# An adaLN block on one core: a new instruction order from planned times, the first x loads on SyncE, a shorter warm-up, and the GpSimd normalisation as product and sum

## The chip, the cores and the metric

The kernel runs on one core of a Trainium2 chip. The metric is device time in microseconds, from the chip's own measurement, as a median over repeated runs. The profile records one execution: instructions by engine (PE is TensorE's matmuls, PEld its weight loads, DVE VectorE, ACT ScalarE, POOL GpSimd, SP SyncE), DMA activity, and the TensorE clock that was granted.

## The reference, cut to what matters

x has 2048 rows of D = 640 bf16 values; c is one row of 640 that conditions the whole block.

```python
mod = (silu(c) @ w_mod).reshape(1, 6, 1, 640)        # w_mod: 640 x 3840
sa, ca, ga, sb, cb, gb = (mod[:, i] for i in range(6))
h = layernorm(x) * (1 + ca) + sa
q, k, v = split_heads(h @ wqkv)                      # 32 heads of 20
p = softmax(where(0 <= i - j < 256, q @ k.T / sqrt(20), -1e9))
x = x + ga * ((p @ v) @ wo)
h = layernorm(x) * (1 + cb) + sb
out = x + gb * ((sigmoid(h @ w_gate) * (h @ w_up)) @ w_down)   # F = 1536
```

The attention is a sliding window: each row sees itself and the 255 rows before it.

## The kernel before, in words

The 2048 rows are worked in 8 chunks of 256 (CH), each of two blocks of 128 rows. The kernel doesn't write its instructions directly. Each piece of work is recorded as an operation with possible engines, an assumed duration and latency, what it reads and writes, a priority and a tag. `Prog.schedule` then places all operations: at each step it takes, for every engine, the earliest possible start, and among those that could start within a small margin of it (PE_EPS on TensorE) the one with the lowest priority number. The table PRI adds a correction by tag. `emit` writes the result: one fixed order per engine, with semaphore waits. On the chip every engine works strictly in that order, SyncE's DMA issues too.

**Conditioning.** c is loaded on ACT's queue, transposed by a small matmul (L624), and turned into silu(c) (L626 to L628). L630 copies it 128 columns wide into silubc. The slices of w_mod go through TensorE with silubc as operand: the first pair (shift and scale of the first layer norm) into tile S at the start (tag modA), the others later (modb, modc). They borrow the space of wd, wu and hh, so those weights can only be loaded afterwards.

**Warm-up.** Until the first modulation weights are there, TensorE runs matmuls on a zeroed buffer (L639, 9 groups of two), and single ones between the modA steps (`fill`, L650).

**First layer norm and projections.** x blocks 0 and 1 are loaded on ACT's queue behind c, all others on SyncE's. `ln_stats` computes mean and variance on VectorE (L741, L743), variance to the power -1/2 on GpSimd (L746, L748), and the normalised x on VectorE or GpSimd (L751). The result is transposed, for chunks 0 and 1 by TensorE (evicted with scale and shift, L786, L787) and afterwards by DMA transposes on SyncE (L757), then scaled and shifted in place (`modulate`, L765, L766, any of three engines). q, k and v come from 320-column matmuls (helper L658); q and k are evicted into stg (L812, L813) and transposed to QT and KT.

**Attention.** There are 90 score sets. A set (`score_set`) is 2048 score columns in the one tile S, four PSUM banks, computed in four strips of TensorE at once (L659), followed by one exponential of 2048 columns on ACT (L924) into one of eight E buffers and by masks on GpSimd (L932, L934). After the sets of half the heads of a chunk, `burst` does P·V into two of the four M banks; `norm` divides on VectorE (transposes L975, reciprocal L980, product L982, transpose L984). The result goes to DRAM (doc<-On) and back in another layout (oT<-doc), both on SyncE.

**Output projection and MLP.** `outproj` multiplies oT by wo, which was scaled by ga, adds x (L1038), and does the second layer norm, with DMA transposes into h2T. `mlp` does gate and up (L658), tanh on ACT (L1078), the product on VectorE (L1080), the down projection with wd scaled by gb, the residual add (L1099) and the store. All projections, P·V groups and MLP tiles share the four M banks.

The priorities let the order mix chunks: while chunk a's score sets run, TensorE's other work is projections of later chunks and output projection and MLP of earlier ones.

Of the kernel before, what the change touches and what calls it, by code (L numbers as in the profile page):

```python
# [8 lines left out]
ALU = mybir.AluOpType  # L9
# [71 lines left out]
class Prog:  # L81
# [3 lines left out]
    def __init__(self, nc):  # L85
        self.nc = nc
        self.ops = []
        self.seq = 0

    def op(self, eng, fn, dur, reads=(), writes=(), prio=50.0, lat=0.05, work=None, tmin=0.0, extra=(), tag="", hold=(),  # L90
# [10 lines left out]
        o.lat = lat  # L101
        o.prio = prio + PRI.get(tag, 0.0)
# [292 lines left out]
def c_pe(n):  # L395
# [3 lines left out]
PE_EPS = 0.117  # L399
PRI = {  # L400
    "amodu2": 349.1, "amodu3": 69.8, "amodu4": -2, "amodu5": 20.4, "amodu6": 21.9, "amodu7": 33.4, "apow0": -17.1,
    "apow1": -0.2, "apow2": -233.1, "apow3": -9.4, "apow4": -4.7, "apow5": -39.6, "apow6": -201.2, "apow7": 26.9,
    "astats1": 2, "astats2": -137.3, "astats3": 147.7, "astats4": 52, "astats5": 202.7, "astats6": 112.2,
    "astats7": -8.8, "atr3": -6.2, "atr4": -3.2, "atr5": -194.6, "atr6": 10.3, "atr7": -24.5, "axh0": -203,
    "axh2": -66.7, "axh3": 71.6, "axh4": -24.4, "axh5": 33.9, "axh6": -20.5, "axh7": 9.8, "bmodu0": -166.8,
    "bmodu1": 13.9, "bmodu2": 1.5, "bmodu3": 15.4, "bmodu4": -1.8, "bmodu5": 93.1, "bmodu6": 3.4, "bmodu7": -1.2,
    "bpow0": 4.3, "bpow1": 150.8, "bpow2": -11.8, "bpow3": -188.6, "bpow4": -35, "bpow5": 41.6, "bpow6": -22.5,
    "bpow7": -15.1, "bstats0": 20.1, "bstats1": 21.9, "bstats2": 16.8, "bstats3": 14.9, "bstats4": 25.8,
    "bstats5": -84.4, "bstats6": 22.4, "bstats7": -22.6, "btr0": -39.2, "btr1": -39.3, "btr2": -8.5, "btr3": 35,
    "btr5": -82, "btr6": 4.1, "btr7": -2.4, "bxh0": 24.8, "bxh1": -260.1, "bxh2": -55.1, "bxh3": 34, "bxh4": 72.4,  # L410
    "bxh5": 103.8, "bxh6": 81, "bxh7": 17.1, "divide_0": -16.1, "divide_1": 34.3, "divide_2": -154.9,
    "divide_3": 6.6, "divide_4": 14.8, "divide_5": -19.9, "divide_6": -11.9, "divide_7": 6.6, "down0": -15.1,
    "down1": -21.3, "down2": -20, "down4": 0.4, "down5": 1.9, "down7": 60.2, "evqk0": 16.1, "evqk1": 334.5,
    "evqk2": 27.2, "evqk3": 339.9, "evqk4": -0.3, "evqk5": 4.1, "evqk6": -33, "evqk7": -0.3, "evqt0": -11.6,
    "evqt1": -8.4, "evv0": 41.8, "evv1": 235.3, "evv2": 2.5, "evv3": -5.5, "evv4": -16.9, "evv5": -108.2,
    "evv6": -60.1, "evv7": -59.5, "exp0": -116.1, "exp1": -16.2, "exp2": -46.3, "exp3": 5.9, "exp4": -147.4,
    "exp5": -3.4, "exp6": 1.1, "exp7": -126.7, "glu_0": -1.3, "glu_1": 0.5, "glu_2": 26.7, "glu_3": -19.5,
    "glu_4": -37, "glu_5": -3.6, "glu_6": 8.5, "glu_7": 4.2, "hTe0": -31.6, "hTe1": 34.3, "mask0": 136.2,
    "mask2": -61.4, "mask3": 78.7, "mask4": -36.4, "mask5": -30.5, "mask6": 3.2, "mask7": 94.8, "mlpg0": -25,
    "mlpg1": -24.5, "mlpg2": -24, "mlpu0": -25, "mlpu1": -24.5, "mlpu2": -24, "modb": -25.7, "modc": -22.2,  # L420
    "n_ow_0": -20.3, "n_ow_1": -41.5, "n_ow_2": 44.8, "n_ow_3": 103.9, "n_ow_4": -5.8, "n_ow_5": -19.8,
    "n_ow_6": -1.4, "n_ow_7": 33.8, "oT_0": 17.5, "oT_1": 32.5, "oT_2": 12.6, "oT_3": 76.6, "oT_4": -64.2,
    "oT_5": 13.2, "oT_6": 2.6, "oT_7": 49.3, "out": 7.2, "projk0": -33.4, "projk2": 26.4, "projk3": -3.9,
    "projk4": 15.6, "projk5": 1.5, "projk6": 7.4, "projk7": 4, "projq0": -114.6, "projq2": 45.3, "projq3": -8.2,
    "projq4": 6.1, "projq5": -4, "projq6": 8.5, "projq7": -7.9, "projv0": -43.1, "projv1": 8.7, "projv2": 224.6,
    "projv4": -6, "projv5": 2.7, "projv6": 16.2, "projv7": 10.7, "ptr0": -337.9, "ptr1": -256.9, "pv0": -37.3,
    "pv1": -290.4, "pv2": -37.9, "pv3": -37.1, "pv4": -28.1, "pv5": -70.8, "pv6": -10.1, "pv7": -9.1, "qkt2": 7.9,
    "qkt3": 6.7, "qkt4": 64.8, "qkt5": -12.3, "qkt6": -3.6, "qkt7": -4.9, "qtr0": -154.4, "qtr1": -20.9,
    "recip_1": -1.9, "recip_2": 23.6, "recip_3": -2.4, "recip_4": 28.1, "recip_5": -22.7, "recip_6": 2.1,
    "recip_7": -9.2, "res1_0": -0.2, "res1_1": 5, "res1_2": 55.2, "res1_3": 7.6, "res1_4": 13.1, "res1_5": -5.3,  # L430
    "res1_6": -6.4, "res1_7": 11.2, "res2_0": 6.2, "res2_1": -29.9, "res2_2": -5.9, "res2_3": 1.7, "res2_4": -3.1,
    "res2_5": 40.9, "res2_6": -17.8, "res2_7": 2.6, "score0": -287.1, "score1": -347.7, "score2": -20.2,
    "score3": 1.8, "score4": -13.1, "score5": -50.5, "score6": -2.7, "score7": 11.5, "tanh_0": 29, "tanh_1": 20.7,
    "tanh_2": 23.5, "tanh_3": 22.7, "tanh_4": 26.2, "tanh_6": -2.3, "tanh_7": -20.3, "tr1_0": 19.8, "tr1_1": 6.2,
    "tr1_2": -28.1, "tr1_3": 15.6, "tr1_4": 45.4, "tr1_5": -90.8, "tr1_6": -19.7, "tr1_7": 5.2, "tr2_0": 204.6,
    "tr2_1": 224.6, "tr2_2": -128.4, "tr2_3": 42, "tr2_4": 64.5, "tr2_5": 40.4, "tr2_6": 0.1, "tr2_7": 27.5,
    "wd": -19.6, "wds": -7.7, "wg": 2.8, "wm2": -13.2, "wo": -20, "wo0": -2.2, "wo1": -12.2, "wo2": 9.1, "wo4": 10.8,
    "wo5": 28.7, "wo6": 6.6, "wo7": 30, "wos": -29.2, "x10": 529.8, "x11": 584.9, "x12": 476, "x13": 633,
    "x14": 745.4, "x15": 731.1, "x4": 394.6, "x5": 337, "x6": 375.5, "x7": 0.5, "x8": 473.6, "x9": 471.4, "y0": 10.9,
    "y1": 23.7, "y10": 8.6, "y11": 0.3, "y12": 0.2, "y13": 31.2, "y14": 1, "y15": 2.7, "y2": -0.2, "y3": 0.4,  # L440
    "y4": 24.5, "y5": 24.4, "y6": 15.9, "y7": -3, "y8": 23.9, "y9": 2,
}
TR1 = 2
# [4 lines left out]
PACE0 = -95.83  # L448
PACE = 0.103
AFTER = 0  # L450
LEAD = 2
FILL = 1
# [8 lines left out]
MOE = ('dve', 'act', 'pool')  # L461


def build(nc, A_x, A_wqkv, A_wo, B_x, B_w_gate, B_w_up, B_w_down, c, w_mod, out, S=2048):
# [50 lines left out]
    p_st = sbpool("st", 3, [128, 32], F32)  # L515
# [51 lines left out]
    def load_x(pool, b, prio, tmin=0.0, eng="sp"):  # L567
        t = Tile(pool, f"{pool.name}_{b}")
        dma(lambda: t.ap[:], lambda: x_flat[b * 128:(b + 1) * 128, :], 0.47 if b > 1 else 0.9, writes=[t.r()], prio=prio, tmin=tmin, tag=f"x{b}" if pool is p_x0 else f"y{b}",
            eng=eng, lat=0.05 if b > 1 else 1.2)  # L570
        return t
# [8 lines left out]
    def load_wm(i, kt, prio, tmin=0.0):  # L580
        if i:
            raise AssertionError
        return dma(lambda: wm_ap[i][:, kt, :], lambda: wm_src[:, kt, i * 1280:(i + 1) * 1280], (1.12 - 0.06 * kt if kt < 4 else 1.2), writes=[Rm[i][kt]],
                   prio=prio, tmin=tmin, tag=f"wm{i}")
# [184 lines left out]
    def pe_transposes(src, dst, sc, sh, Rmod, prio, a):  # L769
        for dt in range(NDT):  # L770
# [9 lines left out]
            if a == 0 and dt == 3:  # L780
                fills.append(fill(2 * FILL, [o]))

# [399 lines left out]
```

The softmax here doesn't subtract the row's maximum and nothing guards it: scores larger than these inputs give would overflow.

## Time and profile before

| | |
|---|---|
| median of 13 runs | 339.74 us (337.82 to 467.41) |
| the profiled execution | 467.41 us, its span 464.4 us |
| granted TensorE clock in it | 0.658 of full, mean |
| busy: PE, PEld | 459.9 us, 277.7 us |
| busy: ACT, DVE, POOL | 234.3, 223.2, 183.6 us |
| exponentials (L924) | 90, 169.0 us, 1.878 us each |
| DMA | 38.72 MB, mean 83 GB/s; 301 GB/s in the first 13.3 us |

The execution that the profiler took is the one of 467.41 us in the list of times; its TensorE clock was at about two thirds from the first microseconds on. Durations on ACT, DVE and POOL don't depend on that clock; those of matmuls do. The busy time of PE is that of pipelined matmuls, so groups of short matmuls overlap in it.

### The profile page before, as it was taken

Reading aid. Unit: us, or ns where it says so; the run is one execution under the profiler, and the core shown is the slowest. Engines: PE = TensorE matmul, PEld = TensorE weight load, DVE = VectorE, ACT = ScalarE, POOL = GpSimd, SP = SyncE. Lnnn points to the kernel's source line nnn. Section 1 sums busy time; section 2 is a strip of 40 time slices with the busy share of each in tenths; the row PEclk is TensorE's granted clock in tenths of the full one; section 3 lists DMA queues with packets and bytes.
Section 4 is the critical chain, followed back from the end, with each engine's and each line's share of the span. In section 5 each row is a group of like instructions: output and inputs, shape, how many; then the busy total and the mean of one; then the engine's idle time right before and its main releaser. Section 6 shows DMA issues by size and latency. Waiting matters only on the chain.

```text
span 464.4 us, 10118 instructions
## 1 busy us (share of the span) xinstructions
PE 459.9 (99%) x4145; PEld 277.7 (60%) x4146; DVE 223.2 (48%) x441; ACT 234.3 (50%) x220; POOL 183.6 (40%) x255
## 2 busy tenths in 40 slices
PE   8999999999999999999999999999999999999997
PEld 3665455556655566555665555665666676765775
DVE  4485756665684451446652465142637424221221
ACT  1675777567663666465866457654576111210110
POOL 3049594545492644344545254343536100100000
PEclk8666666666666666666666666666666666666666
DMA  8869665469102530036402141001210220100000
GB/s 289 291 216 244 238 121 123 113 73 275 61 16 64 93 83 25 29 89 104 96 20 61 38 112 33 18 16 31 68 32 16 68 62 1 28 1 28 30 0 28
DMA packets 71686, 38.72 MB, mean 83 GB/s; under 512 B 46682, under 2 KB 68442, under 8 KB 71642
## 3 DMA queue, kind: packets, MB, share of 16 engines
q1 hardware_dynamic: 71344, 37.76, 32.5%
q8 instruction: 32, 0.52, 0.5%
q10 hardware_dynamic: 298, 0.33, 0.2%
q14 instruction: 12, 0.10, 0.1%
HBM read 21.96 MB, written 5.24 MB: 59 GB/s over the span
## 4 chain that ended last, share of the span: by engine, by line
PE 99%; DVE 0%; issue 0%; ACT 0%
PE M L658 82%; PE S L659 8%; PE M L659 7%; PE S L639 2%; PE S L658 1%; PE S L650 0%; ACT KT L812 0%; DVE stg L813 0%; DVE E L634 0%; DVE x L1099 0%; PE M L624 0%; ACT stg L812 0%
## 5 line engine op out<-in xcount | busy, mean ns | idle before, releaser
L924 ACT ACTIVATE E<-S 128x2048 bf16<-128x2048 f32 x90 | 169.0, 1878 | 91.6 <-PE S L659 89.7
L932 POOL TENSOR_SCALAR_AFFINE_SELECT E<-E 128x512 bf16<-128x512 bf16 (+2 forms) x90 | 77.0, 856 | 163.4 <-ACT E L924 163.2
L658 PE MATMUL M<-h2T,wu 128*128 128x256 bf16 x480 | 89.1, 346 | 0.0
L658 PE MATMUL M<-h2T,wg 128*128 128x256 bf16 x480 | 89.0, 345 | 0.0
L1080 DVE SCALAR_TENSOR_TENSOR hh<-sig,M 128x512 bf16<-128x512 f32 x48 | 33.0, 687 | 100.4 <-PE M L658 89.5
L658 PE MATMUL M<-wd,hh 128*128 128x320 bf16 (+2 forms) x396 | 81.1, 380 | 0.0
L658 PEld LDWEIGHTS M<-h2T,wu 128*128 128x128 bf16 x480 | 56.2, 119 | 22.0 <-issue 2.9
L658 PEld LDWEIGHTS M<-h2T,wg 128*128 128x128 bf16 x480 | 54.4, 117 | 23.5 <-issue 4.4
L1078 ACT ACTIVATE sig<-M 128x512 f32<-128x512 f32 x48 | 28.6, 596 | 78.8 <-PE M L658 78.5
L934 POOL TENSOR_SCALAR_AFFINE_SELECT E<-E 128x512 bf16<-128x512 bf16 (+1 forms) x84 | 67.7, 806 | 0.0
L658 PEld LDWEIGHTS M<-wd,hh 128*128 128x128 bf16 x396 | 44.3, 116 | 32.2 <-issue 2.6
L659 PE MATMUL S<-QT,KT 20*128 20x256 bf16 (+1 forms) x960 | 41.0, 268 | 0.0
L1099 DVE TENSOR_TENSOR x<-M,x 128x320 bf16<-128x320 f32 (+2 forms) x33 | 15.9, 480 | 48.3 <-PE M L658 48.0
L658 PE MATMUL M<-wk,hT 128*128 128x320 bf16 x160 | 36.6, 384 | 0.0
L658 PE MATMUL M<-wq,hT 128*128 128x320 bf16 x160 | 36.2, 385 | 0.1
L658 PE MATMUL M<-wv,hT 128*128 128x320 bf16 x160 | 35.7, 374 | 0.0
L658 PE MATMUL M<-wo,oT 128*128 128x320 bf16 x160 | 34.8, 388 | 0.0
L975 DVE STREAM_TRANSPOSE T<-M 128x512 f32<-128x512 f32 x32 | 21.2, 697 | 26.0 <-PE M L659 26.0
L659 PEld LDWEIGHTS S<-QT,KT 20*128 20x128 bf16 x960 | 14.0, 92 | 30.5 <-issue 26.2
L659 PE MATMUL M<-E,V 128*32 128x256 bf16 (+1 forms) x960 | 31.3, 300 | 0.0
L659 PEld LDWEIGHTS M<-E,V 128*32 128x32 bf16 x960 | 24.3, 113 | 9.1 <-issue 3.3
L741 DVE BATCH_NORM_STATS2 st<-x 128x6 f32<-128x320 bf16 x64 | 28.2, 478 | 1.6 <-DMA x<-in_A_x_dram 1.2
(76 smaller groups left out, 339.3 us busy)
## 6 DMA issues: line engine op xcount, KB each, us to landing
x<-in_A_x_dram SPq DMA_DIRECT2D x30, 160.0 KB
doc<-On SPq DMA_DIRECT2D x64, 40.0 KB
out_dram<-x SPq DMA_DIRECT2D x15, 160.0 KB
wg<-in_B_w_gate_dram SPq DMA_DIRECT2D x5, 384.0 KB
wu<-in_B_w_up_dram SPq DMA_DIRECT2D x5, 384.0 KB
wd<-in_B_w_down_dram SPq DMA_DIRECT2D x4, 480.0 KB
wd<-in_w_mod_dram SPq DMA_DIRECT2D x5, 320.0 KB
wu<-in_w_mod_dram SPq DMA_DIRECT2D x5, 320.0 KB
```

The source lines that it names most:

```text
L639: ins = e.matmul(p_S.aps[0][:, 3, :], Eall[:, 0, 0:128], Eall[:, 0, 128:640], start=True, stop=True)
L658: return e.matmul(o, l, r, start=st, stop=sp, skip_group_check=True)
L659: return e.matmul(o, l, r, start=st, stop=sp, tile_position=tp, skip_group_check=True)
L741: A("dve", lambda e, g, bi=bi, j=j: e.bn_stats(v(bi * 12 + j * 6, 6), src[bi].ap[:, j * 320:(j + 1) * 320]), 0.48, reads=[src[bi].r()], wr ...
L924: A("act", lambda e, eng: e.activation(E.ap[:], Sp.ap[:], ACT.Exp, scale=SM_SCALE), 1.876, reads=[Sp.r()], writes=[E.r()], prio=3, tag=f"e ...
L932: return e.affine_select(ap, ap, pattern=[[0, ap.shape[1]], [1, 128]], compare_op=ALU.is_ge, fill=0.0, base=0, channel_multiplier=-1)
L934: return e.affine_select(ap, ap, pattern=[[0, ap.shape[1]], [-1, 128]], compare_op=ALU.is_ge, fill=0.0, base=-1, channel_multiplier=1)
L975: A("dve", lambda e, g, h=h: e.transpose(T1.ap[:, 512 * h:512 * h + 512], X[h].ap), 0.694, reads=[X[h].r()], writes=[T1.r(h)], prio=3.5, t ...
L1078: A("act", lambda e, g, pg=pg, sg=sg: e.activation(sg.ap[:], pg.ap[:], ACT.Tanh, scale=0.5), c_act(512), reads=[pg.r()], writes=[sg.r()], ...
L1080: A("dve", lambda e, g, pu=pu, sg=sg, f0=f0: e.scalar_tensor_tensor(out=hh.ap[:, f0:f0 + 2, :], in0=sg.ap[:].rearrange("p (a b) -> p a b", ...
L1099: A("dve", lambda e, g, ps=ps, bi=bi, c0=c0, n=n: e.tensor_tensor(x1[bi].ap[:, c0:c0 + n], ps.ap[:, 0:n], x1[bi].ap[:, c0:c0 + n], op=ALU. ...
```

## The change

Nothing of what is computed changes. What does:

- x blocks 0 and 1 are loaded on SyncE's queue, ahead of the w_mod slices; ACT's queue issues only c.
- silubc is copied in two halves. modA and modc need only the first; modb needs both. The statistics of the second x block come after the first half by an added dependency.
- The warm-up has 5 groups of two instead of 9; `fill` is two matmuls instead of one, and the last one also follows the last modA step.
- Where x is normalised, two one-column GpSimd operations first compute -mean times the reciprocal deviation, and the normalisation is x times one column plus the other, on either engine, instead of subtract and multiply.
- The division's first transpose takes both M banks in one instruction (TR1 = 1), instead of one each.
- The planner's assumed durations and latencies of DMAs and of a few operations are changed, and priorities come from a table PLAN of a start time per operation (in tenths of a us, by tag and count), with PRI as a smaller correction. PACE, which spaces the score sets in the planner, goes from 0.103 to 1.822 us. With it the order on all engines is a different one.

```diff
@@ Prog.op
+        k = self.count.get(tag, 0)
+        self.count[tag] = k + 1
+        if tag in PLAN:
+            prio = 0.1 * PLAN[tag][min(k, len(PLAN[tag]) - 1)]
         o.prio = prio + PRI.get(tag, 0.0)
...
-PE_EPS = 0.117
+PE_EPS = 0.11
 PRI = {
...
+PLAN = {
...
+    "score0": [161, 187, 220, 245, 269, 324],
+    "exp0": [168, 199, 224, 249, 273, 329],
...
-TR1 = 2
+TR1 = 1
...
-PACE0 = -95.83
-PACE = 0.103
+PACE0 = -67.17
+PACE = 1.822
...
-FILL = 1
+FILL = 2
...
-    p_st = sbpool("st", 3, [128, 32], F32)
+    p_st = sbpool("st", 3, [128, 34], F32)
...
-    x0[0], x0[1] = load_x(p_x0, 0, 0, eng="act"), load_x(p_x0, 1, 0, eng="act")
+    x0[0], x0[1] = load_x(p_x0, 0, 0), load_x(p_x0, 1, 0.1)
...
-    A("dve", lambda e, g: e.tensor_copy(silubc[:], siluc[:].unsqueeze(2).to_broadcast([128, NDT, 128])), 0.8,
-      reads=[R_siluc], writes=[R_silubc], prio=0)
+    o_sb = A("dve", lambda e, g: e.tensor_copy(silubc[:, :, 0:MW], siluc[:].unsqueeze(2).to_broadcast([128, NDT, MW])), 0.45,
+             reads=[R_siluc], writes=[R_silubc], prio=-1)
+    R_silub2 = R("silub2")
+    A("dve", lambda e, g: e.tensor_copy(silubc[:, :, MW:128], siluc[:].unsqueeze(2).to_broadcast([128, NDT, 128 - MW])), 0.45,
+      reads=[R_siluc], writes=[R_silub2], prio=9, tag="silub2")
...
-    for i in range(9):
+    for i in range(5):
         o = A("pe", warm, 0.85 if i < 4 else 0.43, prio=90, reads=[R_z], extra=wprev, tag="warm", writes=[R("w")])
...
+                  extra=[o_sb] if ln == "a" and a == 0 and bi == 1 else ())
...
+                A("pool", lambda e, g, bi=bi: e.tensor_scalar(st.ap[:, 32 + bi:33 + bi], v(24 + 2 * bi, 1), v(30 + bi, 1), -1.0,
+                                                              op0=ALU.mult, op1=ALU.mult), 0.25,
+                  reads=[st.r("r"), st.r(("m", bi))], writes=[st.r(("n", bi))], prio=1, tag=f"{ln}pow{a}")
+
+                def xh(e, g, bi=bi):
+                    return e.tensor_scalar(dst[bi].ap[:], src[bi].ap[:], v(30 + bi, 1), v(32 + bi, 1), op0=ALU.mult, op1=ALU.add)
...
-                fills.append(fill(2 * FILL, [o]))
+                fills.append(fill(FILL, [o, oA[-1]]))
```

## The prediction

> **What bounds the kernel now.** I read the engine table and the clock row first. The profiled execution took 467.41 us around a span of 464.4 us, with TensorE granted about 0.66 of its clock; the median of the runs is 339.74 us. The page therefore shows a kernel held by TensorE alone:
>
> ```profile
> PE 459.9 (99%) x4145; PEld 277.7 (60%) x4146; DVE 223.2 (48%) x441; ACT 234.3 (50%) x220; POOL 183.6 (40%) x255
> PEclk8666666666666666666666666666666666666666
> ```
>
> To learn what a full clock would leave, I took the chain that ended last, in order of time, for its last stretch:
>
> ```profile
> 356.33 0.40 PE S L659 x16
> ...
> 366.30 95.53 PE M L658 x552
> 461.83 0.02 issue
> 461.85 0.29 DVE x L1099
> ```
>
> Those 552 matmuls stream 149,760 columns (36x320+12x192+12x128 in the last down-projection, 360x256, 132x320), so 1,568 columns a us at a granted 0.65, which is 2,400 at 1.0. I count all columns in the built order with score and P·V matmuls at a quarter (four strips run side by side): 701,824, or 292.4 us at 2,400. At the median's span (339.74 less the 3.0 us that lie around the span) of 336.7 us, TensorE would be idle for 44 us, provided the clock is full there. So something else holds the median. The timeline of one score set shows what:
>
> ```profile
> 22.63 0.40 PE L659 MATMUL S<-QT,KT 20*128 20x256 bf16 x8
> 23.23 1.87 ACT L924 ACTIVATE E<-S 128x2048 bf16<-128x2048 f32 x1
> 25.30 0.42 PE L659 MATMUL S<-QT,KT 20*128 20x256 bf16 x8
> ```
>
> There is one score tile S (four banks), so scores and exponential alternate: exp 1.88, 0.20 until the next score starts, 0.60 until its exp starts, of which 0.33 is streaming at 0.65 clock and 0.21 at full: 0.48. One turn costs at least 1.88+0.20+0.48=2.56 us, and 90 turns 230 us. While they last, TensorE does the other work in the gap; what isn't placed there is done after the last score, with nothing beside it.
>
> **The sum for the kernel before, at full clock.** Between consecutive scores I take the largest of 2.56, the columns placed there over 2,400, and 1.98 plus the other ACT work queued there (evictions 0.44 and 0.60, tanh 0.60, modulation 0.57). Over the 89 intervals this is 247.8 us. After the last score stand 164,608 columns, 68.6 us. The first score comes at 22.63 in the profile, 9.26 us after the first projection (13.37) with TensorE back to back: at full clock 13.37+6.0=19.4. From TensorE's end (461.83) to the span's end are 2.6 us. 19.4+247.8+68.6+2.6=338.4 against 336.7: the picture accounts for the median, so I use differences of it.
>
> **The skill.** The Trainium skill, "Trainium Kernel Development and Optimization", Key Constraints: DMAs issued from SP, ACT and POOL run on the same 16 DMA engines; several issuers save only issue time. The trace agrees: 90% DMA share in the first 13.3 us, at 301 GB/s. "TensorE: Matmul & The Clock Gate", What's actually happening: the first 3.4 us or so of activity run at half clock. Here the first 512-column matmuls took 0.52 us each and later ones 0.3. "SBUF — State Buffer", SBUF: two separate sides: GpSimd and some VectorE operations lock one port pair for a whole instruction; no line before shows that wait apart.
>
> **The change, part by part.**
>
> *Order.* The largest part. Before the first score 29,888 columns stand instead of 31,936; between the scores 535,488 instead of 505,280; after the last score 134,400 instead of 164,608. The tail falls by 30,208 columns, 12.6 us. The same interval sum gives 254.4 instead of 247.8, +6.6: many gaps get work that fits under 2.56 us (unused room 21.7 instead of 29.0 us), but a few are overfull (one of 6.9 us four scores from the end, two of 4.5 in chunk 0). Net -6.0 us. Cost bounds: if nothing that was moved is ready late, -6.0; if each moved column lay openly in the scores' stretch, -12.6+12.6=0; more only if it waits.
>
> *Start.* Two x issues (0.84 us on ACT's queue) move to SP ahead of the five modulation loads (2.29 us), and past wq, wk, wv, which are issued 0.84 later. The bytes up to the last modulation slice are the same, 1.96 MB, and the engines are 90% busy, so that slice lands between 0 and 1.1 us later (0.33 MB at 301 GB/s); x lands sooner (the second now arrives at 7.5, where VectorE waited 1.2 us for it). VectorE's queue now has the first x's statistics ahead of the conditioning step; queued behind them are siluc, silubc and so all modulation matmuls. x is issued at 0.79 with nothing ahead and landed by 5.14 in the old place, so I count no wait. Splitting the copy (0.82 us) lets the first modulation matmul go about 0.4 sooner. Warm-up and fills fall from 24 to 20 matmuls of 512 columns, 0.85 us at full clock. Together between -1.6 and +1.1; I take -0.5.
>
> *Normalisation on GpSimd.* The groups by form:
>
> ```profile
> L932 POOL TENSOR_SCALAR_AFFINE_SELECT E<-E 128x512 bf16<-128x512 bf16 x56 | 37.3, 666 | 92.4 <-ACT E L924 92.4
> L932 POOL TENSOR_SCALAR_AFFINE_SELECT E<-E 128x1024 bf16<-128x1024 bf16 x32 | 35.6, 1114 | 68.3 <-ACT E L924 68.2
> L751 POOL TENSOR_SCALAR x<-x,st 128x640 bf16<-128x640 bf16 x6 | 15.1, 2516 | 0.2 <-issue 0.2
> L766 POOL TENSOR_SCALAR hT<-hT,mA 128x256 bf16<-128x256 bf16 x9 | 5.0, 558 | 0.0
> L746 POOL TENSOR_SCALAR st<-st 128x2 f32<-128x2 f32 x16 | 3.6, 224 | 46.0 <-DVE st L743 46.0
> ```
>
> Subtract-then-multiply on 640 columns takes 2.52 us on GpSimd, yet multiply-then-add on 256 takes 0.56. The new form at 640 isn't in the trace: at most 0.56x2.5=1.4, at least the old floor 0.56; with the masks' slope (0.45 us per 512 columns) 0.56+0.34=0.90, which I take. GpSimd: 6 normalisations of 2.52 become 13 of 0.90 (-3.4), 32 small operations at 0.224 come in (+7.2), 17 modulations become 7 (-5.6): 183.6 becomes 181.8, hidden behind exp as now. Each norm's chain grows by 2x0.224=0.45 us before x can be normalised. That costs nothing while projections and MLP matmuls stand between; without that cover at most 16x0.45=7.2.
>
> *VectorE.* The 32 half-transposes (697 ns) become 16 full ones, between 1.24 (the bf16 row of 1024) and 1.39: 0 to -2.4 us of busy time on an engine at 48%; taken as 0. It also gets 14 more modulations (about 0.4 each, +6) and 7 fewer normalisations (-4): hidden by exp.
>
> Sum: 339.7-6.0-0.5=333.2 us. Of the profiled execution itself (467.41) the same sum says almost nothing changes: at 0.658 clock TensorE is the bound and 2,048 fewer columns are 1.3 us.
>
> **Rivals.**
>
> *Hidden gain.* The moved work comes late by a little. Chunk 0's first MLP matmul stands about 4.7 turns after its output projection, where 5 stood before: some 12.3 us. In the tail the chain from the output projection's end (393.3) to the first modulated h2T (401.8) took 8.5 us; with modulation (1.3), the new small operations (0.45), a mask ahead on GpSimd (1.3) and an exp ahead on ACT (1.9) it is 13.5. That would stall 1.2 us. At 0.7 us a chunk over 8 chunks the gain shrinks by 5.6, to 338.8. For it: shorter cover. Against: later chunks have at least 6 turns.
>
> *Slower.* One mechanism: TensorE runs its order strictly, so an MLP or projection group placed before its h2T or hT is there holds the next score behind it, and ACT misses a turn. Price 2.56 us a time. It decides against the change when the stalls exceed 6.5+1.7 us, so at four missed turns: 10.2-6.5 gives 343.4. For: every interval is fuller, and DMA transposes take 4.1 us from issue (397.73) to use. Against: the covers in the last chunk: 13.1 us of matmuls between P·V and the output projection, where the oT load was issued 8.0 us after P·V (366.3 to 374.25), and 14.1 between projection and MLP for the 8.5+1.3+0.45=10.3 above.
>
> *The change doesn't act.* If the median's clock is not full and TensorE is the bound there too, order can't matter: 339. The sum of 338.4 speaks against it, though it assumes the clock.
>
> **How the numbers follow.** Main case 0.62, 333.2, own range 330.5 to 336.5 (the start's bounds and the unknown GpSimd price). Hidden gain or no action 0.20, around 338.8. Slower mechanism 0.14, 343 and above. More gained than counted 0.04, below 330, if the fuller gaps also remove ACT waits that I charged to both. The range 328.5 to 344 takes these in down to two in ten. A measurement can tell about 0.5% (1.7 us) from no change: below 338.0 is faster, above 341.4 slower. Main, the surplus case and half of the hidden one make 0.76 faster; the rest of the hidden one 0.09 same; 0.15 slower.
>
> **What would show it.** In a profile at full clock: the matmul stretch after the last score near 56 us; exps about 2.6 to 2.8 us apart; GpSimd's 640-column product and sum near 0.9 us; the first projection half a us earlier. ScalarE waiting for scores well past 2.56, with TensorE idle before h2T matmuls, would show the slower rival. The prediction fails most easily if the clock at the median isn't full.

## The result, and where the time went

The changed kernel takes 341.38 us (median of 11 runs, 339.83 to 347.22) against 339.47 us for the kernel before, measured beside it (48 runs). The medians differ by 1.9 us. The ratio, taken without the executions of either kernel that are slow as a whole, is 1.0076 with a 95% interval of 1.0052 to 1.0101: slower by about 2.6 us, where 333.2 was predicted. A second series of the changed kernel (22 runs, beside the last experiment) gave 341.64 us and 1.0080 (1.0055 to 1.0104).

The profile of before that the prediction worked from had a TensorE clock of 0.658, so everything below is compared with a second profile of the kernel before, an execution of 338.04 us with a span of 336.1, which had the full clock. The profiled execution of the changed kernel took 342.46 us, its span 340.7, at a mean clock of 0.995. Engine table and clock row of the page, kernel before:

```profile
PE 326.7 (97%) x4146; PEld 232.5 (69%) x4146; DVE 222.1 (66%) x441; ACT 229.9 (68%) x220; POOL 183.3 (55%) x255
PEclk9999999999999999999999999999999999999999
```

and of the changed kernel:

```profile
PE 327.6 (96%) x4141; PEld 232.5 (68%) x4142; DVE 218.6 (64%) x431; ACT 229.3 (67%) x218; POOL 184.6 (54%) x284
PEclk9999979999999999999999999999999999999999
```

Two things are to be seen. The clock is full, as the prediction needed, but for one slice of the changed kernel (the 7), which is taken up below. And TensorE is 97% busy in the kernel before at that clock, where the prediction had inferred 44 us of idle time from its column count. This is a first sign that an order of work has little to gain. It's no more than a sign, since the profile models the ends of matmuls; the turns below show it.

The last stretch of the chain of work that ended last (start, us, engine, tile, line, number of instructions), kernel before:

```profile
262.74 0.34 PE S L659 x16
263.08 5.11 PE M L658 x38
...
269.62 63.90 PE M L658 x552
```

and the changed kernel:

```profile
280.14 0.34 PE S L1019 x16
280.48 4.78 PE M L1018 x36
...
286.70 51.42 PE M L1018 x436
```

After the last score set (S) 70.4 us of matmuls became 57.6 us: the tail did shrink by about what was predicted. But the last score set now comes 17.4 us later. Cut at the starts of the first and last exponentials, the two spans are:

| stretch | before | after | difference | predicted |
|---|---|---|---|---|
| start to first exponential | 18.6 | 18.4 | -0.2 | -0.5 |
| 89 intervals between exponentials | 244.5 | 262.1 | +17.6 | +6.6 |
| last exponential to the span's end | 73.0 | 60.2 | -12.8 | -12.6 |
| span | 336.1 | 340.7 | +4.6 | -6.5 |

Nearly all of the error sits in the second row. The two profiled executions lie further apart than the medians because that of before fell 1.4 us under its median and that of after 1.1 us above its own.

**What one interval costs.** Intervals are counted from 0. For each of the 89 intervals I took the columns that the built order places there (score and P·V at a quarter, as in the prediction) over 2,400, and subtracted that from the measured interval. The median of what is left is 0.268 us before and 0.273 after. Of the intervals with 1.9 to 2.4 us of columns, 54 of 69 before and 39 of 55 after leave 0.25 to 0.29 us. It is the same 0.26 to 0.27 at 2.13, 2.21 and 2.35 us of columns in both kernels, so it goes with the turn and not with the columns. One turn of the changed kernel, from its timeline (start, us, engine, line, operation; idle before it in brackets):

```profile
209.10 0.40 PE L1019 MATMUL S<-QT,KT 20*128 20x128 bf16 x16
209.44 0.85 PE L1018 MATMUL M<-wo,oT 128*128 128x320 bf16 x5
209.56 1.88 ACT L1295 ACTIVATE E<-S 128x2048 bf16<-128x2048 f32 x1 [0.87 <-PE S L1019]
210.12 0.71 PE L1018 MATMUL M<-wd,hh 128*128 128x320 bf16 x4
210.67 1.11 PE L1018 MATMUL M<-wo,oT 128*128 128x320 bf16 x7
211.71 0.12 PEld L1019 LDWEIGHTS S<-QT,KT 20*128 20x128 bf16 x8 [0.27 <-issue]
211.72 0.40 PE L1019 MATMUL S<-QT,KT 20*128 20x256 bf16 x8
212.16 1.88 ACT L1295 ACTIVATE E<-S 128x2048 bf16<-128x2048 f32 x1 [0.73 <-PE S L1019]
```

The exponential waits 0.73 us for the score. The score waits for no exponential: ahead of it the profile shows only 0.27 us of "issue", time in which the engine waits for nothing that it records. Between the two sets stand 16 matmuls of 320 columns, 2.13 us, plus the set's own 0.21; the turn takes 2.62. TensorE sets the pace, although the columns (2.35) are under the 2.56 that the prediction took for the cost of an exponential's turn.

With the rule "columns plus 0.27, at least 2.38" (the 2.38 is measured below, in the run with the lighter MLP) the intervals add to 236.4 us before and 248.9 after: +12.5. That alone uses up the tail's -12.8. The other 5.1 us of the 17.6 stand above the rule: the intervals exceed it by 8.1 us before and 13.2 after, and 4.5 of these 5.1 stand in the first ten intervals (31.2 us before, 38.3 after). They are waits, and what the waits did to the clock. How much of the 5.1 belongs to the medians, which lie closer together than these two executions, isn't known.

**The early waits.** The timeline of the changed kernel, from its fourth to its seventh score set:

```profile
27.69 0.89 DVE L1101 BATCH_NORM_STATS2 st<-x 128x6 f32<-128x320 bf16 x2 [2.10 <-DMA x<-in_A_x_dram]
28.49 0.48 DVE L1184 CAST stg<-M 128x320 bf16<-128x320 f32 x1
...
29.03 0.45 PE L1018 MATMUL M<-wq,hT 128*128 128x320 bf16 x2 [1.27 <-DVE stg L1184]
...
35.33 1.32 SPq L1128 DMA_TRANSPOSE hT<-x  x1
37.35 1.20 SPq L1128 DMA_TRANSPOSE hT<-x  x1
43.20 1.10 ACT L1136 ACTIVATE hT<-hT,mA 128x256 bf16<-128x256 bf16 x2 [1.74 <-DMA hT<-x]
43.21 0.86 DVE L1137 TENSOR_SCALAR hT<-hT,mA 128x256 bf16<-128x256 bf16 x3 [2.02 <-DMA hT<-x]
43.98 0.69 DVE L1184 CAST KT<-M 128x512 bf16<-128x512 f32 x1
...
44.73 0.40 PE L1019 MATMUL S<-QT,KT 20*128 20x256 bf16 x8 [2.81 <-DVE KT L1184]
```

Two waits of the same kind. First VectorE waits 2.10 us for an x block; the eviction queued behind it (28.49) holds an M bank, and TensorE stands for 1.27. Then both VectorE and ScalarE wait for the DMA transposes of chunk 3's hT, issued at 35.33 and 37.35 and in use only at 43.2. The eviction of KT that chunk 1's first score needs is queued behind them, and TensorE stands for 2.81. The kernel before scales its first hT from DMA transposes on another engine, as its timeline shows:

```profile
38.49 0.40 PE L659 MATMUL S<-QT,KT 20*128 20x256 bf16 x8
...
40.71 1.14 POOL L766 TENSOR_SCALAR hT<-hT,mA 128x256 bf16<-128x256 bf16 x2 [0.51 <-issue]
```

There GpSimd scales at 40.71, nothing of VectorE's stands behind it, and the seventh score set is at 38.49 instead of 44.73. Of these 6.2 us, 2.6 are columns: the changed order puts 18.2 us of them into the first six intervals, the order before 15.5.

**The clock behind a wait.** The 7 in the clock row is one stretch of 3.4 us, from 45.8 to 49.2, right behind the wait of 2.81 us. It shows when busy time is asked for by stretch (stretch; its length; busy time and instructions of PE, PEld, DVE, ACT, POOL; granted clock; DMA). First the changed kernel, then the kernel before:

```profile
45.80:49.20 3.40, 3.40 (x25) 1.97 (x24) 3.05 (x9) 3.18 (x4) 1.22 (x2) 0.50 1.02 356
45.80:49.20 3.40, 3.40 (x59) 2.04 (x57) 2.16 (x5) 3.22 (x3) 3.40 (x5) 1.00 1.38 291
```

The matmuls agree: in the changed kernel's timeline the same group of four transposes takes 0.40 us at 41.51, ahead of the wait, and 0.63 at 47.03.

Intervals 6 and 7, in which the stretch lies, take 6.28 us. In the profile of the run with VectorE's statistics later (below), at full clock, they take 5.08. So 1.2 of the 5.1 us are the clock. In each of the kept profiles, every single wait of TensorE of 2.6 us or more (eight of them, 2.62 to 6.56 us) has such a stretch of 3.4 or 6.8 us at half clock, which begins during the wait or at most 1.1 us behind it. Some shorter waits have one, others (2.24 us in one run) have none. The kernel before waits for 1.48 us at most and has none in its profile.

The same is seen over many executions. In the second series of the changed kernel 7 of 22 had a mean clock of 0.999 or more, with a median of 340.70 us; the other 15 had one of 342.39. Of the kernel before beside it 35 of 43 had such a clock, with a median of 338.88. At full clock the two are 1.8 us apart instead of 2.5. No run varies a wait alone, and the executions at full clock may be those in which the waits were short, so the size is an estimate from these numbers.

### The profile page after: what moved, and what is told of

Its sections match the earlier page's. It is cut to its first block, busy times and chain, and to the rows that moved or that the text cites. A ratio compares the mean times of both kernels' runs of the same rounds, so it can differ in the third digit from the quotient of the medians.

```text
span 340.7 us, 10107 instructions
## 1 busy us (share of the span) xinstructions
PE 327.6 (96%) x4141; PEld 232.5 (68%) x4142; DVE 218.6 (64%) x431; ACT 229.3 (67%) x218; POOL 184.6 (54%) x284
## 4 chain that ended last, share of the span: by engine, by line
PE 81%; DVE 7%; DMA 7%; issue 3%; SPq 1%; ACT 1%; DVEq 0%; ACTq 0%
PE M L1018 67%; PE S L1019 7%; PE M L1019 6%; DMA x<-in_A_x_dram 2%; DVE wd L1435 2%; DMA hT<-x 2%; DMA wd<-in_w_mod_dram 2%; DMA wd<-in_B_w_down_dram 1%; DVE hT L1137 1%; SPq L893 1%; DVE On L1355 1%; ACT E L1295 1%; DVE h2T L1137 1%; DVE hT L1158 0%; DVE V L1184 0%
## 5 line engine op out<-in xcount | busy, mean ns | idle before, releaser
L1295 ACT ACTIVATE E<-S 128x2048 bf16<-128x2048 f32 x90 | 169.0, 1878 | 32.8 <-PE S L1019 29.8
L1018 PE MATMUL M<-h2T,wg 128*128 128x256 bf16 x480 | 71.8, 273 | 1.2 <-DVE hh L1451 1.0
L1018 PE MATMUL M<-h2T,wu 128*128 128x256 bf16 x480 | 72.8, 273 | 0.0
L1018 PE MATMUL M<-wd,hh 128*128 128x320 bf16 (+2 forms) x396 | 56.8, 295 | 0.5 <-DVE x L1409 0.5
L1018 PEld LDWEIGHTS M<-h2T,wg 128*128 128x128 bf16 x480 | 45.3, 98 | 10.0 <-issue 1.5
L1018 PEld LDWEIGHTS M<-h2T,wu 128*128 128x128 bf16 x480 | 44.8, 98 | 9.7 <-issue 3.6
L1018 PE MATMUL M<-wq,hT 128*128 128x320 bf16 x160 | 26.6, 302 | 1.8 <-DVE stg L1184 1.3
L1349 DVE STREAM_TRANSPOSE T<-M 128x1024 f32<-128x1024 f32 x16 | 20.0, 1249 | 11.9 <-PE M L1019 11.6
L1018 PE MATMUL M<-wk,hT 128*128 128x320 bf16 x160 | 27.1, 305 | 0.5 <-DVE T L1349 0.3
L1018 PE MATMUL M<-wv,hT 128*128 128x320 bf16 x160 | 25.4, 300 | 0.0
L1184 DVE CAST stg<-M 128x320 bf16<-128x320 f32 x36 | 17.2, 483 | 8.7 <-PE M L1018 8.5
(78 smaller groups left out, 336.7 us busy)
```

Source lines behind the costliest of these rows:

```text
L1018: return e.matmul(o, l, r, start=st, stop=sp, skip_group_check=True)
L1184: return e.tensor_copy(dst(), src())
L1295: A("act", lambda e, eng: e.activation(E.ap[:], Sp.ap[:], ACT.Exp, scale=SM_SCALE), 1.876, reads=[Sp.r()], writes=[E.r()], prio=3, tag=f"e ...
L1349: A("dve", lambda e, g: e.transpose(T1.ap[:], Mall[:, X[0].slot:X[0].slot + 2, :].rearrange("p a c -> p (a c)")), 1.23, reads=[X[0].r(), X ...
```

## Experiments

The theories go by letters in some of the expectations. **F**: the prediction's floor, an exponential's turn costs at least 2.56 us, and work up to that is free. **P**: TensorE sets the pace in nearly every interval; each costs its columns plus about 0.27 us, so moved work costs its full time. **L**: the loss beyond that comes from loads that arrive late at the head of an evicting engine's queue, between 24 and 45 us. **D**: the loss comes from the denser intervals as such, all along. P and L can both hold, each for its own part of the 17.6 us. In the experiments on order, a helper moves operations in the planned order of one engine and leaves the rest (line numbers shift by up to 27).

### Half of each exponential

The exponential is done on half of the score columns; the other half of E is a constant written once. Half of the exponentials are thus left out.

```diff
-    e.activation(E.ap[:], Sp.ap[:], ACT.Exp, scale=SM_SCALE)
+    e.activation(E.ap[:, :, 0:256], Sp.ap[:, :, 0:256], ACT.Exp, scale=SM_SCALE)
```

> The kernel after with every exponential cut to half its columns (1024 of 2048; the other half of each E buffer is set once at the start and used as it is, so half of the exponentials are left out). The orders stay. Theory F (the floor of the prediction: score, exp and score again set the pace, 2.56 us a turn): the floor falls to about 1.7 us and the span by 15 us or more. Theory P (TensorE sets the pace: an interval is its columns over 2,400 plus 0.27 us that each score set costs on TensorE): the intervals after the first ten keep their lengths within 0.05 us, and the span changes by less than 3 us.

Span 342.0 us (the first exponential comes later, at 23.5, since GpSimd writes the constants first). Groups of ScalarE by form (busy us, mean ns, idle before):

```profile
L1295 ACT ACTIVATE E<-S 128x1024 bf16<-128x1024 f32 x90 | 92.1, 1024 | 66.6 <-PE S L1019 65.0 <-POOL E L1305 1.4
```

and the same turn as shown above, from its timeline:

```profile
210.54 0.40 PE L1019 MATMUL S<-QT,KT 20*128 20x128 bf16 x16
...
213.16 0.40 PE L1019 MATMUL S<-QT,KT 20*128 20x256 bf16 x8
213.60 1.02 ACT L1295 ACTIVATE E<-S 128x1024 bf16<-128x1024 f32 x1 [1.58 <-PE S L1019]
```

77 us of ScalarE's work are gone (169.0 to 92.1), and the turn still takes 2.62 us. The last 30 intervals add to 88.1 us against 88.2, all 79 behind the first ten to 222.9 against 223.8. 62 of these 79 stay within 0.05 us. The one with least columns (1.28 us) falls from 2.41 to 1.56. Where the turn holds its usual columns the exponential bounds nothing: F falls, for the changed kernel. For the kernel before this wasn't run; there the even 0.27 us above the columns says the same.

### Half of the gate and up matmuls

In the changed kernel's own order, only the first of each pair of gate and up matmuls is issued. Half of those two sums is left out.

```diff
-                for k in range(i, j):
+                for k in range(i, i + 1 if gu else j):   # gu: tags mlpg*, mlpu*
```

> The changed kernel in its own order, but of each pair of matmuls of the gate and up projections only the first is issued (five of ten 256-column matmuls for each tile: half of that sum over the inner dimension is left out, 122,880 columns in all). About 30 intervals between scores then hold only 1.17 to 1.28 us of columns. The floor of the prediction (one exponential's turn costs at least 2.56 us) gives 2.56 there, also in full gaps nothing below it, and 245 us for all intervals as worked out. If TensorE sets the pace and 2.56 is no floor: these intervals fall to the true turn of the exponential, which lies at or below the 2.38 that the shortest intervals show, 2.1 to 2.4; intervals whose columns didn't change stay as they are; all intervals together lose 10 to 16 us from 262.1, and the stretch after the last score loses 13.2 of 60.2.

Span 329.0 us, clock 0.968. Two turns with little TensorE work, from its timeline:

```profile
130.06 0.40 PE L1019 MATMUL S<-QT,KT 20*128 20x256 bf16 x8 [0.90 <-ACT E L1296]
...
130.51 1.88 ACT L1296 ACTIVATE E<-S 128x2048 bf16<-128x2048 f32 x1
...
132.44 0.40 PE L1019 MATMUL S<-QT,KT 20*128 20x256 bf16 x8 [0.90 <-ACT E L1296]
...
132.89 1.88 ACT L1296 ACTIVATE E<-S 128x2048 bf16<-128x2048 f32 x1
```

Here the score does wait for the exponential, 0.90 us, and the turn is 2.38: 1.88 of exponential, 0.05 to the next score, 0.45 to the next exponential. Of 31 intervals with less than 1.6 us of columns, 21 lie between 2.37 and 2.41 and none below. So a floor exists, at 2.38 and not 2.56. With P's rule, 81 of the 89 intervals of the kernel before lie above it, 84 after, and the room left under it is 1.8 us in all, before and after. My expectation of the total was wrong: the intervals lost 3.7 us instead of 10 to 16, and the last stretch (60.2 to 52.3) 7.9 instead of 13.2. The chain of this run has tanh (0.61 us a tile) between the thinned gate and up groups of the last stretch, and the load and scaling of wd on it earlier; with less matmul work other waits come forward, and TensorE spends six stretches of 3.4 us at half clock (one in the changed kernel). It measures the floor, not the price of the moved work.

### x blocks 4 and 5 earlier on SyncE

```diff
+    put(P, "sp", [("x4", 0), ("x5", 0)], after=("wm1", 4))   # ahead of wo and wm2
```

> The kernel after with two SyncE issues moved: x blocks 4 and 5 go directly behind the last wm1 slice, ahead of wo and the first two wm2 slices. All other orders stay. Theory L: the blocks land at about 25 us instead of 27.6 and 30.4, VectorE's statistics no longer wait 2.1 and 1.0 us, the exps at 25.9 to 36.9 move up, and the time falls by 2 to 4 us, less if the hT transposes that land at 43.1 then hold the chain anyway (0 to 1). Rival D: no change within 1 us.

342.58 us, ratio 1.0091 (1.0054 to 1.0128), span 340.4. VectorE no longer waits for x, interval 3 falls from 4.82 to 3.38 us. But interval 5 grows from 8.27 to 10.68. Its timeline:

```profile
43.07 0.86 DVE L1151 TENSOR_SCALAR hT<-hT,mA 128x256 bf16<-128x256 bf16 x3 [4.20 <-DMA hT<-x]
...
44.58 0.61 PE L1033 MATMUL S<-QT,KT 20*128 20x256 bf16 x8 [5.00 <-DVE KT L1198]
```

What was won is waited for at the next place: hT still lands at 43, VectorE waits for it for 4.20 us instead of 2.02, and TensorE for 5.00 instead of 2.81. The score set's 0.61 us instead of 0.40 is the half clock again, here from 41.2 to 48.0.

### VectorE's statistics of x later

```diff
+    put(P, "dve",  [("astats2", k) for k in range(6)], after=("evqk1", 2))   # behind the evictions of chunk 1
+    put(P, "dve",  [("axh2", 0)],       after=("tr2_0", 0))
+    put(P, "pool", [("apow2", k) for k in range(4)] + [("axh2", 0)], after=("mask0", 4))
```

> The kernel after with the statistics of x blocks 4 and 5 moved down in VectorE's queue, behind the q and k evictions that stood behind them, and the GpSimd steps of that norm moved behind the next mask. Loads stay where they are. Theory L: evictions no longer stand behind a late load, so the score sets around 28 us come 2 to 4 us earlier; the wait for the transposed hT at 43.1 stays, so the whole gains 0 to 3 us. Rival D: no change within 1 us, or slower.

341.76 us, 1.0078 (1.0052 to 1.0104); the profiled execution, 1.3 us below the median, has a span of 338.7 and 35.6 us in the first ten intervals. Against the changed kernel's own ratio of 1.0076 no gain can be measured. Again the wait for hT remains (intervals 4 and 5: 6.31 and 8.18 us).

### The transposes of hT earlier

Two runs on top of the earlier x blocks. In the first the two DMA transposes go ahead of two of the five wm2 slices on SyncE; in the second behind all five, but ahead of the gate weights, and the scalings go behind an eviction.

```diff
+    put(P, "sp", [("atr3", 0), ("atr3", 1)], after=("wm2", 2))          # first run
+    put(P, "sp", [("atr3", 0), ("atr3", 1)], after=("wm2", 4))          # second run
+    put(P, "dve", [("amodu3", k) for k in range(3)], after=("evqt1", 2))               # second run
+    put(P, "act", [("amodu3", k) for k in range(2)], after=("evqt1", 2))               # second run
```

> As the run with x blocks 4 and 5 moved up, and the two DMA transposes of chunk 3's hT moved up on SyncE from behind three wg slices to behind the third wm2 slice. Theory L: both waits of the stretch go (the 3.1 us for x and the 2 us for hT, with the k evictions behind them), the first ten exp intervals lose 5 to 7 us of their sum, and the time falls by 5 to 7 us to about 335. Rival D: at most 1 us, since the gaps stay as full as they were.

> The kernel after with x blocks 4 and 5 ahead of wo and wm2 on SyncE, the two transposes of chunk 3's hT behind the last wm2 slice instead of between wg slices, and that hT's modulation moved behind the k eviction that stood behind it on VectorE and on ACT. Theory P, with the loss in the first ten intervals: the transposed hT lands by 38 to 40 instead of 43.1, the sixth exp interval falls from 8.3 to below 5, the first ten sum to 32 to 34 instead of 38.3 and the time falls by 3 to 6 us, to 335.5 to 338.5; everything after stays. If the loss is spread over the dense gaps instead: less than 1 us.

Both are slower: 345.46 us, 1.0186 (1.0131 to 1.0241), and 345.80 us, 1.0180 (1.0111 to 1.0249). In the first the modulation weights in hh are late; its timeline:

```profile
40.77 0.96 PE L1032 MATMUL M<-hh,silubc 128*128 128x320 bf16 x3 [5.57 <-DMA hh<-in_w_mod_dram]
```

In the second the first score of chunk 1 does come early, and then x is late; its timeline:

```profile
40.67 0.40 PE L1033 MATMUL S<-QT,KT 20*128 20x256 bf16 x8 [0.47 <-DVE KT L1198]
...
45.59 1.88 SPq L907 DMA_DIRECT2D x<-in_A_x_dram  x2
...
49.45 0.89 DVE L1115 BATCH_NORM_STATS2 st<-x 128x6 f32<-128x320 bf16 x2 [5.29 <-DMA x<-in_A_x_dram]
...
53.28 1.51 PE L1032 MATMUL M<-wq,hT 128*128 128x320 bf16 x5 [6.56 <-DVE stg L1198]
```

In each run another load is late, behind the others on one queue: hT, then hh by 5.57 us, then x by 5.29, for which TensorE stands 6.56 (interval 8 is 10.58 us there). Both runs, like the one with x alone, have 6.8 us at half clock in their profiles, the changed kernel 3.4, so part of their loss is the clock. L holds as to where TensorE stands. But in these runs advancing one load on SyncE's queue only chose which one is late.

### The waiting work away from the evictions

Now the loads stay as they are, and only who waits for them changes. First, chunk 3's scalings go to GpSimd, which is idle then:

```diff
+    to_pool(P, "amodu3", after=("mask0", 5))   # five scalings, from VectorE and ScalarE
```

> The changed kernel, with only the five in-place scalings of chunk 3's hT moved from the heads of VectorE's and ScalarE's queues to GpSimd, directly behind the masks of chunk 0's last set, where GpSimd is idle from 40.85 to 47.12; nothing else in the order. This is the engine on which the kernel before does it. If the early loss comes from evictions of K standing in VectorE's and ScalarE's queues behind scalings that wait for the DMA transposes (landing near 43.1), the KT evictions no longer wait for them, the first score of chunk 1 comes at about 41 to 42 instead of 44.73, the interval before it falls from 8.27 to 5.5 to 6.5, and the span from 340.7 to about 338 to 339. Price of the edit: chunk 3's hT is ready at about 46 (43.1 plus five times 0.57) instead of 44.3, up to 1 us of wait for its projections. If the first 50 us are limited by what the DMA queue delivers, whichever queue waits, the interval falls but those behind it grow by the same, the first ten stay near 38 us together and the span stays within 1 us of 340.7.

342.1 us, 1.0092 (1.0067 to 1.0116), span 340.5. Its timeline:

```profile
42.34 0.40 PE L1032 MATMUL S<-QT,KT 20*128 20x256 bf16 x8
...
43.89 2.69 POOL L1150 TENSOR_SCALAR hT<-hT,mA 128x256 bf16<-128x256 bf16 x5 [2.69 <-issue]
...
48.37 1.28 DVE L1114 BATCH_NORM_STATS2 st<-x 128x6 f32<-128x320 bf16 x3 [3.31 <-DMA x<-in_A_x_dram]
...
50.56 0.85 PE L1031 MATMUL M<-wq,hT 128*128 128x320 bf16 x5 [1.65 <-DVE stg L1197]
```

Interval 5 falls to 5.54 us, as L said (5.5 to 6.5), and the score comes at 42.34. But VectorE, earlier by as much, waits 3.31 us for chunk 4's x, with the next eviction behind it; interval 8 grows from 2.68 to 4.39. The first ten intervals hold 37.3 us instead of 38.3, and the measured time isn't shorter.

So, together: chunk 3's scalings on GpSimd, and the statistics of chunks 2 and 4 behind the evictions.

```diff
+    to_pool(P, "amodu3", after=("mask0", 5))
+    put(P, "dve",  [("astats2", k) for k in range(6)], after=("evqk1", 2))
+    put(P, "dve",  [("axh2", 0)],       after=("tr2_0", 0))
+    put(P, "pool", [("apow2", k) for k in range(4)] + [("axh2", 0)], after=("mask0", 4))
+    put(P, "dve",  [("astats4", k) for k in range(6)], after=("evqk3", 1))
+    put(P, "pool", [("apow4", k) for k in range(4)],   after=("mask1", 7))
```

> The changed kernel with every early wait for a load taken off the heads of the queues that evict: VectorE's statistics of chunk 2 behind the evictions of chunk 1 (with its normalisation and GpSimd's small operations), those of chunk 4 behind the first two evictions of chunk 3, and chunk 3's scalings on GpSimd. Loads and TensorE's order are as they were. If waits for loads at queue heads are what the first ten intervals lost beyond their columns (38.3 measured, 26.8 of columns and 2.7 of fixed cost), most of the rest comes back: the first ten fall to 31 to 34, the span from 340.7 to 334 to 337, the median from 341.4 to 336 to 338, at or below the kernel before. If TensorE's own order needs what the DMA queue delivers late (hT of chunk 3, x of chunk 2), whichever engine waits for it, the first ten stay at 35 to 38 and the span at 338 to 341.

> The changed kernel itself, beside the combination on the same chip: 341.4 as before, within 0.3%; intervals 3 to 6 again hold about 22 us together.

The combination: 340.94 us (22 runs), ratio 1.0038 (1.0016 to 1.0060). The changed kernel beside it: 341.64 us, 1.0080 (1.0055 to 1.0104). About half of the loss is gone; of the two outcomes expected, it is nearer the second. But 20 of its 22 executions had a mean clock of 0.999 or more, against 7 of 22 beside it, and at such a clock the medians are 340.66 and 340.70 us. So as far as these executions tell, the gain is the half-clock stretch that no longer comes, and not the waits themselves. Timeline of the combination:

```profile
40.92 0.40 PE L1046 MATMUL S<-QT,KT 20*128 20x256 bf16 x8
...
42.02 2.87 POOL L1164 TENSOR_SCALAR hT<-hT,mA 128x256 bf16<-128x256 bf16 x5 [2.77 <-issue]
...
44.95 1.94 PE L1045 MATMUL M<-wq,hT 128*128 128x320 bf16 x13 [0.63 <-POOL hT L1164]
```

No eviction stands behind a wait for a load between 34 and 52 us, and the first score of chunk 1 is at 40.92. The first ten intervals hold 36.3 us (profiled execution of 340.84 us), still 6.1 above the rule, where the kernel before is 3.6 above; interval 9 has grown from 2.59 to 4.54. TensorE itself now waits for hT (0.63). The changed kernel's own profile in this series, of an execution of 346.12 us, has two stretches at half clock, and intervals 3 to 6 hold 23.8 us instead of the 22 expected. No order that was run beats the kernel before, and what an order with all early loads in time would give stays open.

### The normalisation's form, alone and taken back

In the changed kernel, the normalisation goes back to subtract and multiply (order and small operations kept):

```diff
-    e.tensor_scalar(dst, src, v(30 + bi, 1), v(32 + bi, 1), op0=ALU.mult, op1=ALU.add)
+    e.tensor_scalar(dst, src, v(24 + 2 * bi, 1), v(30 + bi, 1), op0=ALU.subtract, op1=ALU.mult)
```

> The kernel after with the normalisation back as subtract and multiply, all orders and the small GpSimd steps kept. Thirteen GpSimd operations should take 2.5 instead of 0.87 us, 21 us more busy time on GpSimd. Theory P: masks come late where a normalisation stands ahead of them, P.V groups wait, 2 to 8 us slower. If GpSimd is hidden throughout: within 1 us.

348.67 us, 1.0259 (1.0204 to 1.0313), span 347.4. By the ratios this is 6.2 us more than the changed kernel, by the medians of the two series 7.3. Its timeline:

```profile
56.90 5.01 POOL L1118 TENSOR_SCALAR x<-x,st 128x640 bf16<-128x640 bf16 x2
...
65.23 2.75 PE L1019 MATMUL M<-E,V 128*32 128x256 bf16 x64 [1.95 <-POOL E L1305]
```

Two normalisations of 2.5 us stand ahead of the masks on GpSimd, and P·V on TensorE waits 1.95 us for the masks; that interval is 6.03 us instead of 2.55. The same happens at 184.43 (2.89 us of wait, 7.37 us instead of 3.02). With both comes a stretch of 3.4 us at half clock, so part of the loss is the clock.

The other way round, the new form alone in the kernel before. Its order is kept, with 6 of the normalisations on GpSimd and 26 on VectorE; the 32 small operations stand on GpSimd behind the powers:

```diff
-    e.tensor_scalar(dst, src, v(24 + 2 * bi, 1), v(30 + bi, 1), op0=ALU.subtract, op1=ALU.mult)
+    e.tensor_scalar(dst, src, v(30 + bi, 1), v(32 + bi, 1), op0=ALU.mult, op1=ALU.add)
...
+    e.tensor_scalar(st.ap[:, 32 + bi:33 + bi], v(24 + 2 * bi, 1), v(30 + bi, 1), -1.0, op0=ALU.mult, op1=ALU.mult)
```

> The kernel before with the normalisation as product and sum alone: the order of everything stays, 32 one-column GpSimd steps are put in behind the powers. Six GpSimd normalisations fall from 2.52 to 0.87 us, the small steps cost 8 us, so GpSimd's busy time falls by 2 us. Theory P: the intervals 5, 7 and 13, where masks stand behind a 2.5 us normalisation and cost 1.2 to 1.6 us each beyond the columns, get shorter and the time falls by 1 to 3 us, to about 337. If the longer chain of each norm (0.5 us) counts for more: 0 to 2 us slower.

338.74 us (20 runs), ratio 0.9983 (0.9960 to 1.0006): no difference that this measurement tells, instead of the gain of 1 to 3 us. Intervals 7 and 13 did get shorter (3.66 to 3.01 and 4.09 to 2.54 us), but 5 and 16 longer (6.78 to 7.38 and 2.76 to 4.12). The form is worth 6 to 7 us in the changed kernel's order, which puts 13 normalisations on GpSimd, and nothing measurable in the order before.

## Why the prediction was wrong, step by step

- **The interval sum is the step that failed**: "this is 247.8 us" became 254.4, because "many gaps get work that fits under 2.56 us (unused room 21.7 instead of 29.0 us)". There was 1.8 us of such room. Two sizes were off in the same direction. The turn was put together as 1.88+0.20+0.48; where the exponential does set the pace, it is 1.88+0.05+0.45=2.38. The 0.20 came from a turn in which TensorE, at 0.66 of its clock, was still at other work when the exponential ended at 25.10, as the timeline of that profile shows:

```profile
24.55 0.82 PE L658 MATMUL M<-ident,x 128*128 128x128 bf16 x6
```

And a turn costs TensorE 0.27 us more than its columns. With both put right, and without the term for ScalarE's other work, the sum gives +12.5 instead of +6.6, which with the tail's -12.8 leaves -0.3: no gain. The prediction's own upper bound, "if each moved column lay openly in the scores' stretch, -12.6+12.6=0; more only if it waits", was what happened, and it did wait. The main case put late loads at nothing; they and the half clock behind them are most of the 5.1 us above the rule.

- **Why the check didn't catch it**: the sum gave 338.4 for the kernel before against 336.7, with terms that erred against each other. Its 19.4 for the first score was 1.5 late (17.91; it took the first projection at 13.37 from the slow profile, and at full clock that stands at 11.55), its intervals 3.0 too long (244.8 from score to score), its tail of 71.2 (68.6 and 2.6) 2.2 short of the 73.4 from the last score's start at 262.74. That it fitted was luck. A total that fits doesn't show that the largest of three terms is the right one in each interval. "TensorE would be idle for 44 us" counted columns and no fixed cost per turn; 90 times 0.27 is 24 of these 44.
- **The tail was right**: -12.6 predicted, -12.8 measured; the matmul stretch was to be near 56 us and is 57.6.
- **The start gained nothing**, within its bounds of -1.6 to +1.1. The first projection stands at 11.54 us (11.55 before, where "half a us earlier" was the sign), the first score at 17.99 (17.91), the first exponential at 18.44 (18.60). There was no wait for x, as counted. But the first x's statistics themselves (3.69 to 4.57 us) stand ahead of siluc, which moves from 4.05 to 4.48, and the first modulation matmul, "about 0.4 sooner", comes at 5.44 instead of 5.22. The later ones wait three times for their slices, 0.16 to 0.42 us. The prediction's 0.52 and 0.3 us for a 512-column matmul mix two measures; from start to start they are 0.40 to 0.43 at first and about 0.33 later in its profile.
- **GpSimd's normalisation was right in size**: 0.90 us predicted, 0.871 measured; 0.224 for the small ones, 0.263 measured; its busy time 184.6 us, where 181.8 was predicted. Groups of the changed kernel by form:

```profile
L1118 POOL TENSOR_SCALAR x<-x,st 128x640 bf16<-128x640 bf16 x13 | 11.3, 871 | 0.2
L1113 POOL TENSOR_SCALAR st<-st 128x1 f32<-128x1 f32 x32 | 8.0, 263 | 1.5
```

  "Hidden behind exp as now" missed what the form makes possible: without it this order would have lost another 6 to 7 us.
- **VectorE**: the full transpose took 1.249 us, inside 1.24 to 1.39. But "hidden by exp" was argued from its 48% of busy time. In the first 50 us the order of its queue, not its load, held TensorE up.
- **The rivals**: "if TensorE is the bound there too, order can't matter: 339" was the better picture, and was set aside because of the sum. It tied this to the clock; the clock was full in nearly every stretch and TensorE the bound all the same. The slower rival named the right family, a late hT that holds the next score, but the wrong holder: not a projection group ahead of the score on TensorE, but K's eviction behind the scalings on VectorE and ScalarE. It took the 4.1 us of the tail for a DMA transpose from issue to use; in the loaded stretch it was 5.8 to 7.9 (37.35 and 35.33 to 43.2).

## What to carry to other kernels

Before work is moved under another engine, measure in a full-clock profile who waits for whom in one ordinary turn: here the exponential waited for the score, and so every moved matmul cost its full time. A floor taken from a profile is tested by halving the work of each of the two engines in turn. In an order that is fixed per engine, put what waits for a load behind the evictions or on an idle engine, and look for the next load that becomes late. Where TensorE waits, look at the granted clock behind the wait too: here a wait of 2.81 us was followed by 3.4 us at half clock.

## What the runs showed of the hardware that I had not expected

- A turn with a score set of 2,048 columns in four strips costs TensorE about 0.48 us beyond its other columns (0.21 by a quarter of the set's columns, plus the median 0.27), in both kernels. The weight-load row shows 0.27 us ahead of the set in which it waits for nothing that the profile shows. Turns that also hold a P·V burst, in narrow tiles too, mostly leave 0.39 to 0.51 us above their columns where TensorE waits for nothing. What the 0.27 consists of wasn't tested.
- Single waits of TensorE of 2.6 us and more (eight in the kept profiles) had 3.4 or 6.8 us at half clock during or behind them, and one whole execution of the kernel before (467.41 us) ran at 0.658.
- On GpSimd subtract-then-multiply of 128x640 bf16 takes 2,508 ns, multiply-then-add 871 ns. On VectorE the latter takes 478 ns.
- Half of an exponential's columns take more than half of the time: 1,024 ns for 1,024, 1,878 ns for 2,048.
